# Gate logits as eight more columns of layer 2, which goes twice over the tokens

## The chip, the core and the metric

The kernel runs on one core of a Trainium2 chip. The metric is the device time of one execution in microseconds (us).

The engines are TensorE (PE in the profile; PEld is its weight load), VectorE (DVE), ScalarE (ACT), GpSimd (POOL) and SyncE (SP), which only issues transfers and reads registers here. Each works through its own instructions in order and waits for the others by semaphores.

## The reference

```python
x = attention(q, k, v)                     # sigmoid attention, 4 x 12 heads, 448 x 64 -> x: 1792 x 768
h = maximum(maximum(x @ w1, x @ w2), x @ w3)   # three projections, 768 x 768 each
y = h @ w_out                              # "layer 2", 768 x 768

logits = y @ w_gate + modality_bias[modality_id]   # 1792 x 8
e_idx = argmax(logits, axis=1)                     # one expert of eight for each token
gate = softmax(logits)[e_idx]
out[token] = gate * (relu(y[token] @ w1[e_idx]) @ w2[e_idx])   # 768 -> 1024 -> 768
```

## The kernel before

**Stages.** Attention, then the projections (`project`: six blocks of 128 output features by two halves of the tokens by three weights), then layer 2 with the routing, then the experts. There are TT = 14 token tiles of 128 tokens, and KB = 6 blocks of 128 features. h stays in SBUF as `hA`, `hB`, features on the partitions.

**Products from two parts.** Layer 2 and the experts multiply in fp32r. `split` makes a rounded copy of a tensor on ScalarE and the remainder on VectorE; a product is three matmuls: high by high, high by low, low by high.

**Gate logits.** During the projections VectorE forms `gw` = w_out @ w_gate (768 x 8) in the background. After the last projection TensorE takes `lgp` = gw^T h in plain fp32 (24 matmul calls, 32 output partitions each), VectorE copies it (`lgT`), and four transposes (`route_T`) turn it so that tokens lie on the partitions. `route_gate` adds the bias and finds expert and gate, `route_rank` counts with matmuls, `route_tiles` forms the experts' numbers of the tiles (`exid`), `route_slots` each token's slot. GpSimd then scatters the token numbers to `slots` in DRAM, in 14 indirect transfers. SyncE reads eight expert numbers from `exid` into registers; only then can it issue the loads of expert weights (`wl`).

**Layer 2.** `layer2(t)` makes 18 pairs of matmuls, 512 and 256 columns with the same weights (a tile of h, split). For the last five tiles (from T0 = 9) it first does the 512 columns of all five, and then the 256 columns of all five, so that the gather of the first 512 columns and the first splits of expert weights (`ahead`) can begin in between. The 512-column sums take the PSUM buffers a0 and a1 in turn, the 256-column sums x0 and x1.

**Stores.** A finished tile goes through one of three buffers `xo[t % 3]` to DRAM, `x2d[0]` (columns 0 to 511) and `x2d[1]` (columns 512 to 767, and the gate in column 768). All these stores, the weight loads and the reading back of `idx` are issued by SyncE, in program order. After each tile from t = 2 on, up to two loads of `wl` follow that tile's stores, until four of the fourteen are left. Two experts' weights are loaded this way: per expert w1 in three pieces and w2 in four.

Of the kernel before, what the change touches and what calls it, by code (L numbers as in the profile page):

```python
# [28 lines left out]
def attn_moe_kernel(  # L29
# [45 lines left out]
    def hold(tag, name, *shape):  # L75
        return pool.tile([128, *shape], F32, tag=tag, name=name)
# [74 lines left out]
    def ps(tag, shape, name):  # L151
        return psum.tile(shape, F32, tag=tag, name=name)
# [211 lines left out]
    with tc.manual_schedule(engines={mybir.EngineType.PE, mybir.EngineType.Activation, mybir.EngineType.DVE, SP}):  # L364
# [109 lines left out]
        def project(fb, half, wi):  # L474
# [15 lines left out]
            if half == 1:  # L490
                used[fb, wi] = step[0]

        for fb in range(KB):
            for half in range(2):
                for wi in range(3):
                    project(fb, half, wi)
                    step[0] += 1
                    background(5.8)
        step[0] += 100
        while bg or bg2:  # L500
            step[0] += 1
            background(999)


        lgp = ps("t", [128, 2, 512], "lgp")
        for kk in range(KB):
            for g in range(4):
                n = min(512, NT - 512 * g)
                nc.tensor.matmul(lgp[32 * g:32 * g + 32, 0, 0:n], gw[:, kk, :], hT[kk][:, 512 * g:512 * g + n],  # L509
                                 start=(kk == 0), stop=(kk == KB - 1))  # L510

        wo_ck = hold("P2a", "wo_ck", 2 * KB * DM)
        wo_rl = [cut(wo_ck, 0, KB, 2, 512), cut(wo_ck, KB * 2 * 512, KB, 2, DM - 512)]
        ck = [cut(wo_ck, 2 * DM * i, 2 * DM) for i in range(KB)]
        hs_ = hold("W0", "hs", 2, 2 * KB * 128)
        hs = [hs_[:, t % 2] if t < TT - 3 else hold(f"S{t - TT + 3}", f"hs{t}", 2 * KB * 128) for t in range(TT)]
        hs = [a.rearrange("p (a k c) -> p a k c", a=2, k=KB) for a in hs]
        xo_ = hold("W1", "xo", 3, XW)
        xo = [xo_[:, i] for i in range(3)]

        def split_h(t):
            for h_, k0, k1 in ((hA, 0, 4), (hB, 4, 6)):
                src = h_[:, :, 128 * t:128 * (t + 1)]
                split(hs[t][:, 0, k0:k1], hs[t][:, 1, k0:k1], src)

        def split_wo(kk):
            for w, src in zip(wo_rl, (wof[kk][:, 0:512], wof[kk][:, 512:DM])):
                split(w[:, kk, 0], w[:, kk, 1], src)

        split_wo(0)  # L530
        split_h(0)
        for kk in range(1, KB):
            split_wo(kk)
        split_h(1)
        lgT = cut(gk, 2 * DM, 512)
        nc.vector.tensor_copy(out=lgT[:, 0:256], in_=lgp[:, 0, 0:256])
        nc.vector.tensor_copy(out=lgT[0:96, 256:512], in_=lgp[0:96, 0, 256:512])


        acc_t = {}  # L540

        def layer2(t, cs=(0, 1), ks=range(KB)):
            if ks[0] == 0:
                for c in cs:
                    acc_t[t, c] = ps_a([128, 512], "acc2") if c == 0 else ps(f"x{t % 2}", [128, DM - 512], "acc2b")
            for kk in ks:
                for n, (a, b) in enumerate(((0, 0), (0, 1), (1, 0))):
                    for c in cs:
                        nc.tensor.matmul(acc_t[t, c], r(hs[t][:, a, kk, :]), r(wo_rl[c][:, kk, b]),  # L549
                                         start=(kk == 0 and n == 0), stop=(kk == KB - 1 and n == 2))  # L550

        def layer2_evac(t, cs=(0, 1)):
            o = xo[t % 3]
            if 0 in cs:
                nc.scalar.activation(out=o[:, 0:512], in_=acc_t.pop((t, 0)), func=ACTF.Copy)
            if 1 in cs:
                nc.vector.tensor_copy(out=o[:, 512:DM], in_=acc_t.pop((t, 1)))

        def layer2_store(t, cs=(0, 1)):
            o = xo[t % 3]  # L560
            if 1 in cs:
                nc.vector.tensor_copy(out=o[:, DM:DM + 1], in_=gate[:, t:t + 1])
            for c in cs:
                nc.sync.dma_start(out=x2d[c][128 * t:128 * (t + 1), :], in_=o[:, XC[c][0]:XC[c][1]])


        ro = [0]

        def tmp(*shape):
            n = 1  # L570
            for d in shape:
                n *= d
            ro[0] += n
            assert ro[0] <= 2 * DM
            return cut(gk, ro[0] - n, *shape)

        lg = tmp(TT, E)
        sh = tmp(TT, E)
        oh = tmp(TT, E)
        ohb = tmp(TT, E)  # L580
# [25 lines left out]

            return a.unsqueeze(1).to_broadcast([128, n, a.shape[1]])

        def route_T():
            for j in range(4):  # L610
                n = 128 if j < 2 else 96
                nc.tensor.transpose(lgp[:, 1, 128 * j:128 * j + n], lgT[0:n, 128 * j:128 * (j + 1)], ident[:n, :n])

        def route_gate():
            T = lgp[:, 1, :].rearrange("p (j g x) -> p g j x", j=4, g=4)
            ve.tensor_tensor(out=lg[:, 0:12].rearrange("p (g j) e -> p g j e", g=3), in0=T[:, 0:3, :, 0:E],
                             in1=bias_t[:, 0:12].rearrange("p (g j) e -> p g j e", g=3), op=ALU.add)
            ve.tensor_tensor(out=lg[:, 12:14], in0=T[:, 3, 0:2, 0:E], in1=bias_t[:, 12:14], op=ALU.add)
# [236 lines left out]
        layer2(0)  # L855
        route_T()
        split_h(2)
        layer2_evac(0)
        route_gate()
        layer2(1)  # L860
        pr, cn = route_rank()
        split_h(3)
        layer2_evac(1)
        layer2_store(0)
        layer2_store(1)
        route_tiles(cn)
        ereg = [nc.values_load(exid[0:1, i:i + 1], engines=(SP,), min_val=0, max_val=E - 1) for i in range(NSTAT)]
        wl = deque()
        for i in range(2):
            raw[i] = raw_tiles(i)  # L870
            wl.extend(load_w1(i, ereg[i]))
            wl.extend(load_w2(i, ereg[i]))

        T0 = TT - 5
        for t in range(2, TT):
            cs = (0, 1) if t < T0 else (0,)
            layer2(t, cs)
            if t + 2 < TT:
                split_h(t + 2)
            layer2_evac(t, cs)  # L880
            layer2_store(t, cs)
            if t == 2:
                route_slots(pr)
            for _ in range(2):
                if len(wl) > 4:
                    wl.popleft()()
            if t == 9:
                nc.sync.dma_start(out=idx, in_=slots.rearrange("(p c) o -> p (c o)", p=128))
        xh = hold("H1", "xh", 2 * (KB + FB) * GT)
        xt.extend(cut(xh, KB * GT * i, KB, GT) for i in range(2))  # L890
# [23 lines left out]
        for t in range(T0, TT):  # L914
            if t < TT - 1:
                layer2(t, (1,))
            else:
                layer2(t, (1,), range(0, KB - 3))
                gather_T(0, 0, "t")
                gather_T(0, 1, "x0")  # L920
                layer2(t, (1,), range(KB - 3, KB))
            layer2_evac(t, (1,))
            layer2_store(t, (1,))
            ahead(min(LA, t - T0 + 1))
# [110 lines left out]
```

## Time and profile before

| | |
|---|---|
| median of 3 runs | 766.97 us (766.82 to 767.5) |
| the profiled execution | 767.15 us, of which the trace spans 765.4 us |
| TensorE, busy share of the span | 99% |
| VectorE, ScalarE, GpSimd | 59%, 34%, 9% |
| granted clock of TensorE, mean | 0.999 |

The span runs from the first to the last instruction. Busy shares are means over stages with different limits. Matmuls are pipelined: a recorded matmul reaches past the start of the next one, so the pace of a run of matmuls is read from the chain, not from the mean duration of one. The expert stage gathers tokens by expert and works through seven full tiles and one half tile.

### The profile page before, as it was taken

To read this page: it belongs to the slowest core of one execution; us is meant where nothing else is said; L and a number is where in the kernel's file an instruction comes from. 1 tells how busy PE (TensorE), PEld (TensorE's weight loads), DVE (VectorE), ACT (ScalarE), POOL (GpSimd) and SP (SyncE) were. 2 spreads that over 40 slices of the span, in tenths; PEclk is the share of its full clock that TensorE was granted. 3 is DMA by queue.
4 is the path that set the end of the run, shared out by engine and by line. 5 is a ranking of instruction groups with operands and counts; after the bars stand their busy time and mean duration, and the time that the engine had idled before them with its cause. 6 is when DMAs were issued, how large, how long until landed. Compare 5 with 4: busy or idle time off the path is not lost.

```text
span 765.4 us, 11862 instructions
## 1 busy us (share of the span) xinstructions
PE 756.1 (99%) x4704; PEld 642.1 (84%) x4704; DVE 449.8 (59%) x754; ACT 258.1 (34%) x362; POOL 67.5 (9%) x84
## 2 busy tenths in 40 slices
PE   8999999999999999999999999999999999999996
PEld 5455544999999999999978888999999989899995
DVE  4677774757779787844137522455556555556542
ACT  4666555001010100100032222354544544454522
POOL 1000000000000000000000420313020202021010
PEclk9999999999999999999999999999999999999999
DMA  9766680132620312200001692452757211064000
GB/s 216 181 168 166 163 226 2 59 108 83 205 79 26 124 62 83 83 2 0 1 1 43 226 395 78 134 196 88 271 193 253 107 29 57 15 249 159 29 26 19
DMA packets 44993, 88.07 MB, mean 115 GB/s; under 512 B 8139, under 2 KB 27100, under 8 KB 44934
## 3 DMA queue, kind: packets, MB, share of 16 engines
q1 hardware_dynamic: 41142, 75.45, 31.2%
q0 software_dynamic: 3632, 11.59, 4.6%
q8 instruction: 39, 0.64, 0.3%
q10 hardware_dynamic: 160, 0.23, 0.1%
q14 instruction: 20, 0.16, 0.1%
HBM read 94.95 MB, written 11.57 MB: 139 GB/s over the span
## 4 chain that ended last, share of the span: by engine, by line
PE 98%; DMA 1%; issue 0%; POOL 0%; SPq 0%; POOLq 0%; DVE 0%; ACT 0%; ACTq 0%
PE acc L483 34%; PE hacc L801 16%; PE oacc L822 15%; PE acc L549 8%; PE X L336 7%; PE s L310 6%; PE acc2b L549 4%; PE X L344 1%; PE hacc L954 1%; PE xT L762 1%; PE s L326 1%; PE oh L969 1%; PE lgp L509 1%; DMA u<-in_qk_dram 1%; PE wgp L352 0%
## 5 line engine op out<-in xcount | busy, mean ns | idle before, releaser
L483 PE MATMUL acc<-xR,w_ring 128*128 128x448 f32 x864 | 210.5, 365 | 0.0
L483 PEld LDWEIGHTS acc<-xR,w_ring 128*128 128x128 f32 x864 | 162.2, 188 | 13.5 <-issue 0.7
L822 PE MATMUL oacc<-wo_ck,xh 128*128 128x512 f32 (+1 forms) x672 | 124.0, 341 | 0.0
L801 PE MATMUL hacc<-xh,wo_ck 128*128 128x256 f32 x1008 | 122.4, 283 | 0.0
L801 PEld LDWEIGHTS hacc<-xh,wo_ck 128*128 128x128 f32 x1008 | 121.9, 192 | 0.3
L822 PEld LDWEIGHTS oacc<-wo_ck,xh 128*128 128x128 f32 x672 | 102.8, 188 | 13.8
L483 PE MATMUL acc<-xLa,w_ring 128*128 128x448 f32 x360 | 102.2, 365 | 0.0
L295 ACT ACTIVATE at<-s,nlns 128x896 f32<-128x896 f32 x84 | 77.9, 1007 | 44.9 <-PE s L310 43.5
L185 DVE TENSOR_TENSOR wo_ck<-raw,wo_ck 128x512 fp32r<-128x512 f32 (+1 forms) x108 | 75.6, 743 | 6.7 <-ACT wo_ck L184 6.6
L549 PE MATMUL acc<-wo_ck,hs 128*128 128x512 f32 x252 | 77.4, 394 | 0.0
L483 PEld LDWEIGHTS acc<-xLa,w_ring 128*128 128x128 f32 x360 | 67.6, 188 | 5.3
L184 ACT ACTIVATE wo_ck<-raw 128x512 fp32r<-128x512 f32 (+1 forms) x108 | 67.1, 671 | 12.4 <-PE hacc L801 12.2
L549 PEld LDWEIGHTS acc<-wo_ck,hs 128*128 128x128 f32 x252 | 47.2, 188 | 11.3 <-ACT wo_ck L184 0.8
L549 PE MATMUL acc2b<-wo_ck,hs 128*128 128x256 f32 x252 | 56.2, 280 | 0.0
L310 PEld LDWEIGHTS s<-kq 64*128 64x128 f32 x432 | 37.6, 184 | 22.1 <-issue 15.5
L310 PE MATMUL s<-kq 64*128 64x448 f32 x432 | 51.2, 377 | 0.9 <-ACT kq L281 0.9
L465 DVE SCALAR_TENSOR_TENSOR gk<-wof,gk 128x768 f32<-128x768 f32 x48 | 45.9, 956 | 1.1
L487 ACT ACTIVATE hA<-acc 128x896 f32<-128x896 f32 x8 | 7.4, 920 | 115.1 <-PE acc L483 115.1
L808 DVE SCALAR_TENSOR_TENSOR xh<-hacc,xh 128x1024 fp32r<-128x1024 f32 x14 | 17.1, 1224 | 45.6 <-ACT xh L807 45.6
L753 POOL DMA_INDIRECT xg<-x2d,idx x30 | 30.3, 1012 | 146.8 <-PE xT L762 99.9
L549 PEld LDWEIGHTS acc2b<-wo_ck,hs 128*128 128x128 f32 x252 | 41.5, 189 | 0.1
L489 DVE TENSOR_TENSOR hB<-hB,acc 128x896 f32<-128x896 f32 x8 | 8.7, 1086 | 50.2 <-PE acc L483 50.2
(182 smaller groups left out, 700.3 us busy)
## 6 DMA issues: line engine op xcount, KB each, us to landing
raw<-in_moe_w_dram SPq DMA_DIRECT2D x24, 1024.0 KB
stage<-in_moe_w_dram SPq DMA_DIRECT2D x18, 768.0 KB
u<-in_qk_dram SPq DMA_DIRECT2D x46, 224.0 KB
raw<-in_moe_w_dram SPq DMA_DIRECT2D x12, 768.0 KB
raw_S<-in_moe_w_dram SPq DMA_DIRECT2D x12, 768.0 KB
stage<-in_moe_w_out_dram SPq DMA_DIRECT2D x6, 768.0 KB
x2d<-xo SPq DMA_DIRECT2D x14, 256.0 KB
gk<-wgT SPq DMA_DIRECT2D x8, 384.0 KB
```

The costliest lines, as they stand in the source:

```text
L184: nc.scalar.activation(out=r(dR), in_=src, func=ACTF.Copy)
L185: nc.vector.tensor_tensor(out=r(dL), in0=src, in1=dR, op=ALU.subtract)
L295: nc.scalar.activation(out=dst, in_=s[:, :, 0:S], func=ACTF.Sigmoid, scale=qscale, bias=nlns)
L310: nc.tensor.matmul(s[g][:, h, 0:S], r(kt[p, a, 0, 128 * g:128 * (g + 1)]), r(kt[p, x, 1]), start=(n == 0), stop=(n == 2))
L336: nc.tensor.matmul(X_t[u][64 * h:64 * h + 64, 0:S], vt[:, 2 * g + h], at[:, 2 * g + h], start=(g == 0), stop=False)
L465: nc.vector.scalar_tensor_tensor(out=junk, in0=wof[kb], scalar=1.0, in1=wgb[e % 2], op0=ALU.mult, op1=ALU.mult, accum_out=gw[:, kb, e:e + 1])
L483: nc.tensor.matmul(acc[:, c, 0:S], r(m[:, a, kk, :]), r(x[kk][:, c0 + S * c:c0 + S * (c + 1)]), start=(kk == 0 and n == 0), stop=(kk == KB ...
L549: nc.tensor.matmul(acc_t[t, c], r(hs[t][:, a, kk, :]), r(wo_rl[c][:, kk, b]), start=(kk == 0 and n == 0), stop=(kk == KB - 1 and n == 2))
L753: nc.gpsimd.indirect_dma_start(out=xg[i % 2][s][:, XC[c][0]:XC[c][1]], out_offset=None, in_=x2d[c], in_offset=bass.IndirectOffsetOnAxis(ap ...
L801: nc.tensor.matmul(acc[:, f], r(w[a][:, 128 * f:128 * (f + 1)]), r(x[:, kk]), start=(kk == 0 and m == 0 and f % 2 == 0), stop=(kk == KB - ...
L808: nc.vector.scalar_tensor_tensor(out=r(dL), in0=src, scalar=0.0, in1=dR, op0=ALU.max, op1=ALU.subtract)
L822: nc.tensor.matmul(dst, r(x[:, f, 128 * s:128 * (s + 1)]), r(w[a][:, c0:c1]), start=(f == 0 and m == 0 and not (shared and s == 1)), stop= ...
```

## The change

The 8 columns of `gw` are appended to the first 256 columns of w_out. Layer 2 goes twice over the tokens.

- **Pass A** (`pass_a`, tokens 0 to 13): 264 columns. ScalarE copies the 256 to `xoa` and they are stored to `x2d[0]`; VectorE adds the 8 logits to the bias in place (`lg`). The sums take x0 and x1. Split tiles of h are kept in buffers of their own; the weights for it are split in S0 to S2 during the last projections, and the other 512 columns' weights (`wo_b`) alongside.
- **Pass B** (`pass_b`, tokens 9 to 13, then 0 to 8): the other 512 columns as one matmul whose moving operand is two runs of 256. It uses the kept splits for the first five positions p and splits again for the nine others. For p = 9 to 13 it takes 256 columns of all five and then the other 256 of all five; both halves take x0 and x1. ScalarE evacuates. The routing runs beside it: `route_gate` after position 0, `route_rank` and `route_tiles` after 1, the loads of expert weights from position 3 on, two after each.
- `lgp`, `lgT` and `route_T` are gone, and the wait for the background work after the projections.

```diff
+        def split_a(i):
+            w = hold(f"S{i}", f"wo_a{i}", 2, 2, NA)              # NA = CA + E = 264
+            wo_a.extend(w[:, k] for k in range(2))
+            split(w[:, :, 0, 0:CA], w[:, :, 1, 0:CA], cut(us[i], 0, 2, DM)[:, :, 0:CA])
+            split(w[:, :, 0, CA:NA], w[:, :, 1, CA:NA], gw[:, 2 * i:2 * i + 2, 0:E])
...
                     background(5.8)
+                    if fb == KB - 1 and half == 1:
+                        split_a(wi)
+                        if wi < 2:
+                            hs1[wi] = hs_view(w_ring_[1][:, 0] if wi == 0 else hold("K1", "hs_k", 2 * DM))
+                            split_h(wi, hs1[wi])
-        lgp = ps("t", [128, 2, 512], "lgp")
-        for kk in range(KB):
-            for g in range(4):
-                n = min(512, NT - 512 * g)
-                nc.tensor.matmul(lgp[32 * g:32 * g + 32, 0, 0:n], gw[:, kk, :], hT[kk][:, 512 * g:512 * g + n],
-                                 start=(kk == 0), stop=(kk == KB - 1))
...
+        wo_b = cut(wo_ck, 0, 2, KB * 2 * CA).rearrange("p c (k a n) -> p c k a n", k=KB, a=2)
...
+        def split_b(kk):
+            split(wo_b[:, :, kk, 0], wo_b[:, :, kk, 1], wof[kk][:, CA:DM].rearrange("p (c n) -> p c n", c=2))
+        def layer2(acc, hs, w, ks=range(KB)):
+            for kk in ks:
+                for n, (a, b) in enumerate(((0, 0), (0, 1), (1, 0))):
+                    nc.tensor.matmul(acc, r(hs[:, a, kk, :]), r(w(kk, b)), start=(kk == 0 and n == 0),
+                                     stop=(kk == KB - 1 and n == 2))
+        def pass_a(t):
+            acc_t[t] = ps(f"x{t % 2}", [128, NA], "acc_a")
+            layer2(acc_t[t], hs1[t], lambda kk, b: wo_a[kk][:, b])
+        def end_a(t):
+            acc = acc_t.pop(t)
+            nc.scalar.activation(out=xoa[t % 2], in_=acc[:, 0:CA], func=ACTF.Copy)
+            nc.vector.tensor_tensor(out=lg[:, t], in0=bias_t[:, t], in1=acc[:, CA:NA], op=ALU.add)
+            nc.sync.dma_start(out=x2d[0][128 * t:128 * (t + 1), 0:CA], in_=xoa[t % 2])
...
+        for t in range(1, TT):
+            pass_a(t)
+            if t + 3 < TT:
+                split_h(t + 3, hs1[t + 3])
+            end_a(t)
+            if t % 2 == 0 and t // 2 <= KB:
+                split_b(t // 2 - 1)
...
+        toks = list(range(9, TT)) + list(range(9))
+        P0 = TT - 5
...
+        def pass_b(p, c=None, ks=range(KB)):
+            if ks[0] == 0:
+                acc_t[p] = ps_a([128, 2, CA], "acc_b") if c is None else ps(f"x{p % 2}", [128, CA], "acc_c")
+            layer2(acc_t[p], hs2[p], (lambda kk, b: wo_b[:, :, kk, b]) if c is None else lambda kk, b: wo_b[:, c, kk, b], ks)
+        def end_b(p, c=None):
+            o, rows = xo[p % 3], slice(128 * toks[p], 128 * (toks[p] + 1))
+            c0, c1 = (CA, DM) if c is None else (CA * (c + 1), CA * (c + 2))
+            nc.scalar.activation(out=o[:, c0:c1], in_=flat(acc_t.pop(p)) if c is None else acc_t.pop(p), func=ACTF.Copy)
+            if c != 1:
+                nc.sync.dma_start(out=x2d[0][rows, CA:512], in_=o[:, CA:512])
+            if c != 0:
+                nc.vector.tensor_copy(out=o[:, DM:DM + 1], in_=gate[:, toks[p]:toks[p] + 1])
+                nc.sync.dma_start(out=x2d[1][rows, :], in_=o[:, 512:XW])
+        pass_b(0)
         route_gate()
+        end_b(0)
+        pass_b(1)
         pr, cn = route_rank()
+        end_b(1)
         route_tiles(cn)
+        pass_b(2)
+        end_b(2)
         ereg = [nc.values_load(exid[0:1, i:i + 1], engines=(SP,), min_val=0, max_val=E - 1) for i in range(NSTAT)]
...
+        route_slots(pr)
+        for p in range(3, TT):
+            c = None if p < P0 else 0
+            pass_b(p, c)
+            if NK <= p + 2 < TT:                                  # NK = 5
+                split_h(toks[p + 2], hs2[p + 2])
+            end_b(p, c)
             for _ in range(2):
                 if len(wl) > 4:
                     wl.popleft()()
-            if t == 9:
+            if p == 8:
                 nc.sync.dma_start(out=idx, in_=slots.rearrange("(p c) o -> p (c o)", p=128))
```

## Rows read from the trace of the kernel before

**Rows 1.** The page, busy time of each engine and share of the span.
```profile
PE 756.1 (99%) x4704; PEld 642.1 (84%) x4704; DVE 449.8 (59%) x754; ACT 258.1 (34%) x362; POOL 67.5 (9%) x84
```
**Rows 2.** The chain that ended last, 396 to 492 us: start, length, what.
```profile
396.21 5.28 PE lgp L509 x30
...
408.05 0.39 PE lgp L612 x4
...
459.18 20.43 PE acc L549 x90
479.61 9.71 PE acc2b L549 x81
489.32 0.93 PE xT L762 x8
...
491.32 10.11 PE hacc L801 x84
```
**Rows 3.** Timeline of VectorE, 396 to 428 us: start, duration, what.
```profile
396.25 1.09 DVE L489 TENSOR_TENSOR hB<-hB,acc 128x896 f32<-128x896 f32 x1 [6.14 <-PE acc L483]
...
415.81 0.15 DVE L654 CAST gk<-rank 128x8 int32<-128x8 f32 x1
...
421.27 0.16 DVE L680 SCALAR_TENSOR_TENSOR exid<-gk 128x1 int32<-128x1 f32 x1
...
422.69 0.17 DVE L686 TENSOR_TENSOR gk<-gk 128x16 f32<-128x16 f32 x1
...
427.82 0.17 DVE L712 SCALAR_TENSOR_TENSOR spos<-gk 128x14 int32<-128x14 int32 x1
```
**Rows 4.** Groups by shape, 396 to 492 us: count, busy us, mean ns, idle before.
```profile
L185 DVE TENSOR_TENSOR hs<-hA,hs 128x512 fp32r<-128x512 f32 x14 | 9.7, 690 | 24.7 <-ACT hs L184 24.6
...
L185 DVE TENSOR_TENSOR hs<-hB,hs 128x256 fp32r<-128x256 f32 x14 | 5.9, 421 | 8.3 <-ACT hs L184 8.3
...
L184 ACT ACTIVATE hs<-hB 128x256 fp32r<-128x256 f32 x14 | 5.8, 413 | 13.1 <-PE acc2b L549 13.1
```
**Rows 5.** Timeline of SyncE's issues, 408 to 464 us.
```profile
421.46 0.26 SPq L682 DMA_DIRECT2D exd<-exid  x1
426.72 0.82 SPq L564 DMA_DIRECT2D x2d<-xo  x2
427.80 1.03 SPq L738 DMA_DIRECT2D raw<-in_moe_w_dram  x2
...
448.34 0.98 SPq L738 DMA_DIRECT2D raw<-in_moe_w_dram  x2
```
**Rows 6.** Stretches: engines' busy us, then granted clock, DMA share, GB/s.
```profile
442.00:446.00 4.00, 4.00 (x25) 3.52 (x24) 0.69 (x1) 0.63 (x1) 2.92 (x4) 1.00 1.04 411
...
458.50:459.00 0.50, 0.50 (x4) 0.41 (x4) 0.00 (x0) 0.13 (x1) 0.00 (x0) 1.00 0.51 168
```
**Rows 7.** DMA issues, 380 to 520 us: count, KB each, us to landing.
```profile
raw<-in_moe_w_dram SPq DMA_DIRECT2D x9, 1024.0 KB
raw<-in_moe_w_dram SPq DMA_DIRECT2D x6, 768.0 KB
x2d<-xo SPq DMA_DIRECT2D x14, 256.0 KB
...
x2d<-xo SPq DMA_DIRECT2D x14, 136.0 KB
...
slots<-tokid,spos POOLq DMA_INDIRECT x14, 5.8
```
**Rows 8.** Timeline of GpSimd, 395 to 500 us: first and last of 14 scatters, first gather.
```profile
428.88 1.07 POOL L715 DMA_INDIRECT slots<-tokid,spos  x1 [45.06 <-issue]
...
445.99 0.97 POOL L715 DMA_INDIRECT slots<-tokid,spos  x1 [0.30 <-issue]
...
483.36 1.00 POOL L753 DMA_INDIRECT xg<-x2d,idx  x1 [36.40 <-DVE wo_ck L185]
```
**Rows 9.** Timeline of ScalarE: the last 512-column evacuation.
```profile
479.70 0.60 ACT L555 ACTIVATE xo<-acc 128x512 f32<-128x512 f32 x1 [3.48 <-PE acc L549]
```

More of the change, by code (lines that the diff above doesn't have):

```diff
@@ L491, in project, with hs_view, split_h @@
                 used[fb, wi] = step[0]
+        CA = 256
+        NA = CA + E
+        wo_a, hs1 = [], {}
+        def hs_view(a):
+            return a.rearrange("p (a k c) -> p a k c", a=2, k=KB)
+        def split_h(t, hs):
+            for h_, k0, k1 in ((hA, 0, 4), (hB, 4, 6)):
+                src = h_[:, :, 128 * t:128 * (t + 1)]
+                split(hs[:, 0, k0:k1], hs[:, 1, k0:k1], src)
+        def split_a(i):
[3 more added lines that the diff above has]
+            split(w[:, :, 0, CA:NA], w[:, :, 1, CA:NA], gw[:, 2 * i:2 * i + 2, 0:E])
         for fb in range(KB):
@@ L498, in attn_moe_kernel @@
                     background(5.8)
[L499 to L502, printed above, removed]
-        lgp = ps("t", [128, 2, 512], "lgp")
-        for kk in range(KB):
-            for g in range(4):
-                n = min(512, NT - 512 * g)
-                nc.tensor.matmul(lgp[32 * g:32 * g + 32, 0, 0:n], gw[:, kk, :], hT[kk][:, 512 * g:512 * g + n],
-                                 start=(kk == 0), stop=(kk == KB - 1))
-        wo_ck = hold("P2a", "wo_ck", 2 * KB * DM)
@@ L513, in attn_moe_kernel @@
[L513 to L537, printed above, removed]
+                    if fb == KB - 1 and half == 1:
+                        assert not bg and not bg2
+                        split_a(wi)
+                        if wi < 2:
+                            hs1[wi] = hs_view(w_ring_[1][:, 0] if wi == 0 else hold("K1", "hs_k", 2 * DM))
+                            split_h(wi, hs1[wi])
@@ new lines, in attn_moe_kernel @@
+        wo_ck = hold("P2a", "wo_ck", 2 * KB * DM)
+        wo_b = cut(wo_ck, 0, 2, KB * 2 * CA).rearrange("p c (k a n) -> p c k a n", k=KB, a=2)
+        ck = [cut(wo_ck, 2 * DM * i, 2 * DM) for i in (0, 1, 4, 5, 2, 3)]
+        hs_w = hold("W0", "hs_w", 2, 2 * DM)
+        hs_p = hold("P1", "hs_p", 7, 2 * DM)
+        hs_r = hold("P2b", "hs_r", 2 * DM)
+        for t in range(2, TT):
+            hs1[t] = hs_view(hs_p[:, t - 2] if t < 9 else hs_w[:, t - 9] if t < 11 else ck[t - 9] if t < 13 else hs_r)
@@ L540, in attn_moe_kernel @@
+        def split_b(kk):
+            split(wo_b[:, :, kk, 0], wo_b[:, :, kk, 1], wof[kk][:, CA:DM].rearrange("p (c n) -> p c n", c=2))
         acc_t = {}
[L542 to L545, printed above, removed]
+        def layer2(acc, hs, w, ks=range(KB)):
             for kk in ks:
                 for n, (a, b) in enumerate(((0, 0), (0, 1), (1, 0))):
-                    for c in cs:
-                        nc.tensor.matmul(acc_t[t, c], r(hs[t][:, a, kk, :]), r(wo_rl[c][:, kk, b]),
-                                         start=(kk == 0 and n == 0), stop=(kk == KB - 1 and n == 2))
@@ L552, in layer2_evac @@
[L552 to L564, printed above, removed]
+                    nc.tensor.matmul(acc, r(hs[:, a, kk, :]), r(w(kk, b)), start=(kk == 0 and n == 0),
+                                     stop=(kk == KB - 1 and n == 2))
@@ new lines, in pass_a @@
+        def pass_a(t):
[6 more added lines that the diff above has]
+            nc.sync.dma_start(out=x2d[0][128 * t:128 * (t + 1), 0:CA], in_=xoa[t % 2])
+        lg = bias_t
@@ new lines, in attn_moe_kernel @@
+        split_h(2, hs1[2])
+        pass_a(0)
+        xo_ = hold("W1", "xo", 3 * XW + 2 * CA)
+        xo = [cut(xo_, XW * i, XW) for i in range(3)]
+        xoa = [cut(xo_, 3 * XW + CA * i, CA) for i in range(2)]
+        split_h(3, hs1[3])
+        end_a(0)
+        for t in range(1, TT):
[5 more added lines that the diff above has]
+                split_b(t // 2 - 1)
+        rt = hold("K1", "rt", 2 * DM)
@@ L574, in tmp @@
             assert ro[0] <= 2 * DM
-            return cut(gk, ro[0] - n, *shape)
-        lg = tmp(TT, E)
+            return cut(rt, ro[0] - n, *shape)
         sh = tmp(TT, E)
@@ L607, in bc1 @@
             return a.unsqueeze(1).to_broadcast([128, n, a.shape[1]])
[L609 to L612, printed above, removed]
         def route_gate():
[L615 to L618, printed above, removed]
             ve.tensor_reduce(out=mx, in_=lg, axis=AX.X, op=ALU.max)
@@ L854, in attn_moe_kernel @@
             nc.sync.dma_start(out=d[NT:NT + 1, :], in_=xo[0][0:1, c0:c1])
[L855 to L858, printed above, removed]
+        NK = TT - 9
+        toks = list(range(9, TT)) + list(range(9))
+        P0 = TT - 5
+        hs2 = [hs1[t] for t in toks[:NK]]
+        hs_s = [hold(f"S{i}", f"hs_s{i}", 2 * DM) for i in range(3)]
+        ring = [hs_view(a) for a in (hs_s[0], hs_s[1], hs_w[:, 0], hs_w[:, 1], hs_s[2])]
+        hs2 += [ring[i % 5] for i in range(9)]
+        def pass_b(p, c=None, ks=range(KB)):
[12 more added lines that the diff above has]
+        pass_b(0)
         route_gate()
-        layer2(1)
+        end_b(0)
+        pass_b(1)
         pr, cn = route_rank()
[L862 to L865, printed above, removed]
+        end_b(1)
         route_tiles(cn)
+        pass_b(2)
+        end_b(2)
         ereg = [nc.values_load(exid[0:1, i:i + 1], engines=(SP,), min_val=0, max_val=E - 1) for i in range(NSTAT)]
@@ L872, in attn_moe_kernel @@
             wl.extend(load_w2(i, ereg[i]))
[L874 to L883, printed above, removed]
+        route_slots(pr)
[5 more added lines that the diff above has]
+            end_b(p, c)
             for _ in range(2):
@@ L912, in ahead @@
                             ld()
-        for t in range(T0, TT):
-            if t < TT - 1:
-                layer2(t, (1,))
+        for p in range(P0, TT):
+            if p < TT - 1:
+                pass_b(p, 1)
             else:
-                layer2(t, (1,), range(0, KB - 3))
+                pass_b(p, 1, range(0, KB - 3))
                 gather_T(0, 0, "t")
                 gather_T(0, 1, "x0")
[L921 to L924, printed above, removed]
+                pass_b(p, 1, range(KB - 3, KB))
+            end_b(p, 1)
+            ahead(min(LA, p - P0 + 1))
         gather(0, ixs[0], (1,))
```

## The prediction

> **What bounds the kernel now.** I read the page first: TensorE is busy for 99% of the span [rows 1], so time can only be won by taking matmuls away and lost by letting TensorE wait. Then the chain that ended last: it is TensorE work almost from end to end, and the change touches the stretch from 396.21 (projections done, gate logits begin) to 491.32 us (first expert matmul), 95.11 us [rows 2]. In it the reader should see the gate logits (5.28 us), their transposes (0.39 us), a run of 90 matmuls of 512 columns, one of 81 matmuls of 256 columns, and the expert's 8 transposes (0.93 us). Then the DVE timeline for the routing chain [rows 3], the groups by shape for the splits [rows 4], SyncE's timeline [rows 5], DMA shares by stretch [rows 6] and issue sizes [rows 7], and GpSimd and ScalarE around the gather [rows 8, 9]. All of these hide behind TensorE today. The question is whether they still do.
>
> **TensorE's own work.** A matmul of 512 columns costs 20.43/90 = 0.2270 us and one of 256 costs 9.71/81 = 0.1199 us, weight load included [rows 2]. The slope is 0.1071/256 = 0.00042 us per column, so one of 264 is 0.1199 + 8 x 0.00042 = 0.1232 us.
> Before: 9 tiles x 18 pairs x 0.3469 = 56.2, five tiles' first 512 columns 90 x 0.2270 = 20.4, their last 256 columns 90 x 0.1199 = 10.8; 87.4 us.
> After: pass A 14 x 18 x 0.1232 = 31.05; pass B 9 x 18 x 0.2270 = 36.77; five tiles in two halves 180 x 0.1199 = 21.58; 89.4 us. That is 90 more matmuls and 8 more columns on 252: +2.0 us.
> Removed: 5.28 + 0.39 = 5.67 us. The rank matmuls, the expert's transposes and small pacing losses stay. Net -3.7 us.
> Not in this trace: pass B's moving operand is two runs of 256 columns that lie apart. Its bounds are one matmul of 512 (0.2270) and two of 256 (0.2398): 0 to +2.1 us. I take 0, as it is one instruction with one weight load.
>
> **Small waits on TensorE.** (a) The third pair of 264-column weights is split on DVE behind the last projection maximum, which ends near 397.3 [rows 3]. Its subtraction (512 wide 0.69, then 16 wide about 0.15 [rows 3, 4]) is done near 398.1; pass A's fourteenth matmul wants it at 396.21 + 13 x 0.1232 = 397.8. About +0.35 us. (b) In the five split tiles both halves now use the buffers x0 and x1. The last first half (p=13) and the first second half (p=9) both take x1, so TensorE waits for one evacuation: a 256-wide ScalarE copy (0.41 [rows 4]) and the hand-over each way, together about +0.6 us. Before, the 512-column half had other buffers. Sum so far: -3.7 + 0.95 = -2.7 us.
>
> **The splits.** Nine tiles are split a second time, and all of pass A's splits sit beside 2.22 us passes. One tile costs DVE 0.69 + 0.42 = 1.1 us [rows 4], with the logit add (about 0.15) and every other step a weight split (0.7): at most 2.0 of 2.22 us. Hidden. If that cover went, the excess would be paid 14 times.
>
> **Routing.** It now starts after pass A, at about 396.2 + 31.05 + 0.35 = 427.6, and pass B sets its cover. The gate chain takes some 4 us (it leads up to the rank matmuls, which come after two passes of 18 x 0.2270 = 4.09: 8.2 us), so the rank matmuls don't wait. From their end, 436.4, the tiles chain takes 421.27 - 415.81 + 0.16 = 5.6 us and the slots chain 427.82 - 422.69 + 0.17 = 5.3 us [rows 3]: 442.2 and 447.5. Queued behind it on DVE is the split for p=5, done at 448.6; its low part is first wanted near 449.0. Just hidden: a slip of 0.5 us costs that slip.
>
> **The loads and stores on SyncE's queue.** This is the step that decides. Before, SyncE sends the expert numbers at 421.46, reads eight registers until the next store at 426.72, and issues the first weight load at 427.80; the tenth goes out by 449.3 [rows 5]. They are six of 1024 KB and four of 768 KB, 9.44 MB [rows 7]. A tile's pair of loads (about 1.9 MB) and its stores (256 + 136 KB) come every 6.24 us, which the DMA engines keep up with: they run full and fall idle near 458.8 [rows 6]. That is 11.4 MB (ten loads, five tiles' stores) in 31 us, 0.367 MB per us from the first load on, scatters included.
> After: exid is ready at 442.2, the stores of p=2 and the register reads (5 us) last to 448.4, the second store of p=3 waits for DVE until 448.9, and the first load goes out at 449.6. A pair now comes with every pass of 4.09 us, but 2.1 to 2.4 MB need 5.2 to 6.4 us. So a backlog grows, and the stores of x2d stand in it: SyncE issues them on the same queue, each behind the loads of the tiles before it.
> Store p=8 (its first part) has 9.44 MB of loads, four tiles' stores (1.08) and its own 0.13 ahead: 10.65 MB / 0.367 = 29.0 us, so its data end at 478.6 and it lands at about 479.6. Store p=7 has 8.29 MB: 22.6 us, landed about 473.2.
> What waits: xo has three buffers. ScalarE's evacuation of p=10's first half writes where store p=7 reads, p=11's where store p=8 reads. Unhindered, the first halves (18 x 0.1199 = 2.16 us) would end at 467.2, 469.3, 471.5, 473.7 and 475.8. p=12 needs p=10's PSUM buffer: free at 473.2 + 0.45 instead of 469.9, so it starts 2.1 us late. p=13 needs p=11's: free at 479.6 + 0.4 = 480.0 instead of a start at 473.7. TensorE is then 6.3 us late in all. Before, the same three buffers wait for nothing, since the last load has landed by 459 and the five halves follow.
> Bounds: DMA at the fullest stretch's 0.411 MB per us [rows 6] gives 25.9 us instead of 29.0 and a wait of 3.2 us; a rate a tenth lower gives 9. I take the measured mean. If a store doesn't stand behind the loads on its queue, the wait is nothing.
> The Trainium skill, "DMA: Bandwidth & Descriptors", section "Queues, rings and completion order", says that each DMA engine consumes the descriptors of a ring in ring order and that SyncE's row has one ring on each engine. By that rule the stores wait as worked out above and the sum is +3.6 us; if they could overtake, it would be -2.7. No row here shows the order of a store and a load; the rows show only that one backlog exists.
>
> **The gather.** The scatters begin at 447.5 + 0.9 = 448.4, last 18.1 us and land 5.8 later [rows 7, 8], about 472; the slot list is then read behind the backlog, near 480. The gather starts 483.36 - 479.61 = 3.75 us after the last first half and the transposes 5.96 us after that [rows 2, 8], of which some is slack. With p=13 ending at 482.2 the gather starts near 486 and the transposes are due at 482.8 + 9.7 = 492.5. Hidden with half a microsecond to spare by that full distance. ScalarE's evacuations are 0.60 us before and shorter after [rows 9].
>
> **Sum.** -3.7 + 0.95 + 6.3 = +3.6 us: 767.15 + 3.6 = 770.7 for an execution like the profiled one, which is 0.2 above the median of the runs: 770.5.
>
> **Rivals.**
> 1. Stores overtake loads, or land in time. Then only TensorE's work counts: 767.0 - 2.7 = 764.3, from 763.2 (no waits at all) to 766.4 (two-run operand at its upper bound). For it: ScalarE never waits for a store in this trace. Against: the backlog is 5 MB here and was under 2 MB there. It decides as soon as store p=8 lands before 473.3 instead of 479.6, that is, with 6.3 us less of backlog.
> 2. The wait is half as large, because the DMA runs at its best rate or the loads go out some microseconds sooner: 767.0 - 2.7 + 3.2 = 767.5. No measurable change.
> 3. The wait costs TensorE its clock as well. It would stand idle for 2.1 and some 4.2 us with 2.2 us of work between. The granted clock is 1.00 in every row here [rows 6] and TensorE has no such gap in this stretch. If the clock fell to its lower level for 2 to 5 us of the work that follows, that work doubles: 772.5 to 775.5. The Trainium skill, "TensorE: Matmul & The Clock Gate", Part 1, has idleness throttle the array to 1.2 GHz; no run here shows it.
> 4. Each added matmul pays an exposed weight load: 90 x about 0.1 = +9 us more. Against it: the 256-column run above already holds one weight load per matmul at 0.1199 us. I leave it 1 in 100.
>
> **Chances.** Forecast (full wait) 0.58; rival 1 0.22; rival 2 0.12; rival 3 0.07; rival 4 0.01. The full wait's own range is 768.3 to 772.0. Taken together 8 in 10 lie between 763.6 and 772.5. A measurement of this kernel tells 0.2% (1.5 us) from no change: faster means under 765.4, slower above 768.5. Rival 1 gives 0.22 less the upper end of its operand cost, rival 2 a little on both sides: faster 0.24, same 0.16, slower 0.60.
>
> **What would show it.** In the profile after: no gate-logit matmuls; 252 matmuls of 264 columns at about 0.123 us each; first load near 449.6; DMA full until about 478; ScalarE standing before the evacuations of p=10 and p=11 for several microseconds with no engine to wait for, and TensorE idle twice between 471 and 480. If TensorE runs through that stretch, the order of the queue is not what I took, and the time is near 764. If the wait sits earlier, at p=5, DVE's routing chain was too long; if at the transposes, the gather was.

## The result and the profile after

| | median us (range, runs) | ratio to before [95% interval] |
|---|---|---|
| before | 767.06 (766.82 to 767.50, 5) | |
| changed | 773.31 (772.13 to 776.44, 5) | 1.0088 [1.0068, 1.0108] |

The change makes the kernel 0.9% slower, 6.25 us by the medians and 2.8 us more than predicted. The profiled execution took 772.55 us. Its span is 770.3 us against 765.4, and its mean granted clock 0.994 where it had been 0.999.

The chain that ended last, of the kernel after (start, length, what):

```profile
397.77 29.21 PE acc_a L546 x239
426.98 8.18 PE acc_b L546 x36
...
435.73 17.65 PE acc_b L546 x78
...
457.49 11.32 DMA x2d<-xo
...
468.88 10.75 DMA x2d<-xo
...
479.73 0.39 ACT xo L872
...
480.17 3.66 PE acc_c L546 x18
...
484.34 9.98 PE acc_c L546 x81
494.32 0.87 PE xT L762 x8
...
496.26 3.77 PE hacc L801 x31
```

The first expert matmul starts at 496.26 and not at 491.32 [rows 2]: 4.94 us, which is the whole difference of the spans. Two stores of x2d (of p = 6 and p = 8), 22 us together, now stand in a chain that was TensorE work almost from end to end. Who waits for them is in ScalarE's timeline (in brackets the idle time before, and what ended it). These are the first halves' evacuations p = 9, 10 and 11:

```profile
468.92 0.38 ACT L872 ACTIVATE xo<-acc_c 128x256 f32<-128x256 f32 x1 [3.00 <-DMA x2d<-xo]
...
473.85 0.38 ACT L872 ACTIVATE xo<-acc_c 128x256 f32<-128x256 f32 x1 [3.72 <-DMA x2d<-xo]
...
479.73 0.38 ACT L872 ACTIVATE xo<-acc_c 128x256 f32<-128x256 f32 x1 [4.68 <-DMA x2d<-xo]
```

TensorE's timeline has the first halves p = 11, 12 and 13 and then the second halves, each behind one of these evacuations, or (the last) behind the turn of x1:

```profile
469.35 2.42 PE L546 MATMUL acc_c<-wo_ck,hs_s 128*128 128x256 f32 x18 [0.63 <-ACT xo L872]
474.28 3.81 PE L546 MATMUL acc_c<-wo_ck,hs_w 128*128 128x256 f32 x18 [2.51 <-ACT xo L872]
480.17 3.65 PE L546 MATMUL acc_c<-wo_ck,hs_w 128*128 128x256 f32 x18 [2.07 <-ACT xo L872]
484.34 6.74 PE L546 MATMUL acc_c<-wo_ck,hs_s 128*128 128x256 f32 x54 [0.52 <-ACT xo L872]
```

The same 18 matmuls take 2.42 us at 469 and 3.8 us at 474 and at 480. The stretches say why (TensorE's busy time and matmuls; then granted clock, DMA share, GB/s):

```profile
472.00:474.00 2.00, 0.00 (x0) 1.00 1.04 424
474.00:476.00 2.00, 1.72 (x8) 0.51 1.03 412
476.00:478.00 2.00, 2.00 (x12) 0.64 1.04 377
478.00:480.00 2.00, 0.10 (x1) 1.00 0.31 109
480.00:482.00 2.00, 1.83 (x11) 0.72 0.26 90
482.00:484.00 2.00, 1.81 (x9) 0.50 0.14 47
```

After each of the two long pauses the granted clock falls to 0.5, that is from 2.4 to 1.2 GHz; after the pause of 0.63 us the 18 matmuls still take 2.42 us. And the DMA engines, which had been idle from 459 on [rows 6], are full until 478.

SyncE's timeline: the first loads, the slowest pair, the last pair, and the store of p = 8:

```profile
448.73 1.03 SPq L738 DMA_DIRECT2D raw<-in_moe_w_dram  x2
...
453.95 3.44 SPq L745 DMA_DIRECT2D raw<-in_moe_w_dram  x2
...
466.79 1.77 SPq L738 DMA_DIRECT2D raw<-in_moe_w_dram  x2
468.88 0.34 SPq L874 DMA_DIRECT2D x2d<-xo  x1
```

The first load goes out 20.9 us later than before [rows 5], and the store of p = 8 right behind the last two.

### The profile page after: what moved, and what is told of

It is laid out like the page before. It is cut to its first block, busy times and chain, and to the rows that moved or that the text cites. A ratio compares the mean times of both kernels' runs of the same rounds, so it can differ in the third digit from the quotient of the medians.

```text
span 770.3 us, 12019 instructions
## 1 busy us (share of the span) xinstructions
PE 755.4 (98%) x4742; PEld 649.6 (84%) x4742; DVE 455.9 (59%) x768; ACT 270.5 (35%) x399; POOL 66.8 (9%) x84
## 4 chain that ended last, share of the span: by engine, by line
PE 94%; DMA 3%; issue 0%; ACT 0%; DVE 0%; POOL 0%; SPq 0%; POOLq 0%; ACTq 0%
PE acc L483 34%; PE hacc L801 16%; PE oacc L822 15%; PE X L336 7%; PE s L310 6%; PE acc_a L546 4%; PE acc_b L546 3%; DMA x2d<-xo 3%; PE acc_c L546 2%; PE X L344 1%; PE hacc L970 1%; PE s L326 1%; PE xT L762 1%; PE oh L985 1%; DMA u<-in_qk_dram 1%
## 5 line engine op out<-in xcount | busy, mean ns | idle before, releaser
L336 PE MATMUL X<-at,u 128*64 128x448 f32 x192 | 37.8, 544 | 0.0
L766 DVE TENSOR_TENSOR xh<-xT,xh 128x512 fp32r<-128x512 f32 x21 | 14.4, 691 | 37.1 <-ACT xh L765 37.1
L489 DVE TENSOR_TENSOR hA<-hA,acc 128x896 f32<-128x896 f32 x16 | 17.4, 1086 | 31.1 <-PE acc L483 30.7
L852 POOL MEMSET xo<- 128x784 f32 x3 | 2.1, 757 | 387.2 <-DVE hs_p L185 387.2
L361 DVE CAST xR<-X 128x448 fp32r<-128x448 f32 x24 | 14.9, 620 | 34.7 <-PE X L344 34.7
```

Of the source, the lines that this page charges most:

```text
L336: nc.tensor.matmul(X_t[u][64 * h:64 * h + 64, 0:S], vt[:, 2 * g + h], at[:, 2 * g + h], start=(g == 0), stop=False)
L489: nc.vector.tensor_tensor(out=dst, in0=dst, in1=acc[:, :, 0:S], op=ALU.max)
```

## The experiments

**Which runs can be compared.** The first four kernels ran on a chip on which the kernel before itself took 772.16 us (769.90 to 775.73, 23 runs). Everywhere else it took 767.0 to 767.4, so the ratios of those four aren't used. All four were run again on other chips (labels with b, below "second"), and the conclusions rest on these. Theory: the stores stand behind the weight loads on SyncE's queue, the three `xo` buffers come free late, TensorE waits, and the clock falls in the waits. Rivals: the bytes have to move in any case, so another order only shifts the wait; or the clock costs nothing, since it falls while TensorE would wait anyway.

**Two marks.** The kernel before, and the changed kernel, each run as a kernel beside others, on two different chips.

> The kernel before, unchanged, run beside the changed one on this chip. No theory is at stake: it should take about 767.0 us, 5 us less than the changed kernel, at a granted clock of 0.999, and it gives the mark that the two kernels below have to pass.

> The changed kernel as it is, on the same chip as the three below, to settle what they are measured against: on one chip so far its profile had no wait of ScalarE for TensorE's signal at 457 to 468, on another four kernels with the same first half of pass B had one of 7 to 8 us. Theory, the difference is the chip's or the execution's: 772 to 774 here, with the waits for the stores of p = 6, 7 and 8 as in the profile after. If the kernel before is near 772 on a chip where the hold-back kernel is at 768, the whole stretch is slower there for both kernels.

Before: 767.41 us (766.73 to 768.90, 11), ratio 1.0005 [0.9996, 1.0014]. Changed: 774.41 us (771.74 to 777.89, 6), ratio 1.0084 [1.0070, 1.0099]. The change costs the same here, and its executions lie 6 us apart where those of before lie 2 apart (3.4 on the chip of the changed kernel, 766.38 to 769.74, 17).

### 1. The stores of the second quarter issued by ScalarE

```diff
-                nc.sync.dma_start(out=x2d[0][rows, CA:512], in_=o[:, CA:512])
+                nc.scalar.dma_start(out=x2d[0][rows, CA:512], in_=o[:, CA:512])
```

> The stores of columns 256 to 511 in pass B are issued by ScalarE instead of SyncE; all else is as in the changed kernel. Theory (a store waits in its queue behind the weight loads issued before it): on a queue without loads they land 2 to 4 us after they are issued, TensorE stands still no more between p=11 and p=13, the clock stays at 1.00 and the time is 764.3, between 763.8 and 765.5. Rival 1 (the 16 DMA engines are full until 478, so any store is late on any queue): much of the wait stays, 767 to 772. Rival 2 (the pair of PSUM buffers x0 and x1, or the late routing, makes the wait): 773 as before the edit.

> The stores of the second quarter issued by ScalarE, so that they don't stand behind weight loads, beside a kernel before at 767. Theory: the first halves no longer wait, as in the run before; but idx and the stores of the last third stay behind the loads on SyncE, the gather comes late, and of the 6.3 us at most 2 to 3 come back: 769 to 771. If the order behind the loads were not the cause, 772 to 774 as the changed kernel.

First chip 771.16 us (769.33 to 773.26, 12). Second 768.27 us (767.30 to 770.64, 12), ratio 1.0015 [1.0005, 1.0025]: 5 us under the changed kernel by the ratios, 6 by the medians, though nothing but the issuing engine differs. TensorE goes from the first halves to the second ones with one wait of 0.47 us; it waits later, for the gathered tokens (TensorE's timeline of the second run, whose profiled execution, 770.55 us, was one of the slower ones):

```profile
489.13 0.33 PE L762 MATMUL xT<-ident,xg 128*128 128x128 f32 x1 [2.19 <-DMA xg<-x2d,idx]
491.26 1.53 PE L762 MATMUL xT<-ident,xg 128*128 128x128 f32 x7 [1.81 <-DMA xg<-x2d,idx]
```

The place behind the loads on SyncE is the cause of the first waits. The edit takes the stores out of two places at once, from behind the loads in the queue and from behind SyncE's own waiting issues (see the last section), and doesn't tell one from the other. In this execution 4 us come back as a wait for the gather; what the gather waits for last is `idx`, which SyncE issued at 476.18 and which landed at 484.47. The time missed both expectations: it is above the 764.3 of the first and under the 769 to 771 of the second. It lies in the range of rival 1 (767 to 772), which is right in part: the store of p = 8, issued by ScalarE at 467.17, landed at 473.5, after 6.3 us and not 2 to 4, where on SyncE it landed at 479.6.

### 2. Buffers of their own for the five first halves

```diff
-        rt = hold("K1", "rt", 2 * DM)
+        rt = hold("K1", "rt", 3 * DM)
...
+            d = o[:, c0:c1] if c != 0 else h0[p - P0]
-            nc.scalar.activation(out=o[:, c0:c1], ...
+            nc.scalar.activation(out=d, ...
-                nc.sync.dma_start(out=x2d[0][rows, CA:512], in_=o[:, CA:512])
+                nc.sync.dma_start(out=x2d[0][rows, CA:512], in_=d[:, 0:CA])
...
+        h0 = [cut(rt, 2 * DM + CA * i, CA) for i in range(3)] + xoa
```

> The five first halves are evacuated into five buffers of their own (256 columns each) instead of into xo; every store stays on SyncE's queue, as late as it is. Theory (the late stores cost time only because ScalarE may not write xo before they have read it): no wait in the first halves; what is left is the gather, which has to wait for the last of these stores near 480 and then has 6 us until the transposes fall due near 486: 764.3 to 765.5. Rival 1 foretells the same here. Rival 2: 773 as before the edit.

> The five buffers of their own for the first halves and nothing else: ten loads, stores behind them as in the changed kernel. Theory, late stores hurt through the buffers alone: no first half waits though its predecessors' stores land as late as before, TensorE runs through to the second halves, 764 to 765.5. Rival, the late stores hold up the gather as well: in the changed kernel the last second halves came late themselves; here they come 6 us sooner, and if the stores of the second halves then stand behind what is left of the loads, xT waits for xg and 767 or more is left. The waits of ScalarE for xo of p = 4 and 5 (evacuations p = 7 and 8) stay in either case.

First chip 767.37 us (766.62 to 769.55, 6). Second 766.18 us (765.90 to 770.07, 11), ratio 0.9997 [0.9986, 1.0008]. The stores are as late as ever, and no first half waits. What is left in TensorE's timeline is the turn of x1 and, again, the gather:

```profile
475.80 6.74 PE L546 MATMUL acc_c<-wo_ck,hs_s 128*128 128x256 f32 x54 [0.47 <-ACT xo L873]
...
486.25 0.33 PE L762 MATMUL xT<-ident,xg 128*128 128x128 f32 x1 [0.48 <-DMA xg<-x2d,idx]
488.04 0.98 PE L762 MATMUL xT<-ident,xg 128*128 128x128 f32 x7 [1.46 <-DMA xg<-x2d,idx]
```

So a late store costs through the buffer that it holds, and with that gone through the gather: both sides of the expectation were partly right.

### 3. Idle matmuls in the two long pauses

```diff
             c = None if p < P0 else 0
+            if p >= TT - 2:
+                if p == TT - 2:
+                    idle = ps("t", [128, 2, 512], "idle")
+                for i in range(20 if p == TT - 2 else 28):
+                    nc.tensor.matmul(idle[:, 0, 0:CA], r(hs2[9][:, 0, 0, :]), r(wo_b[:, 0, 0, 0]), start=True, stop=True)
             pass_b(p, c)
```

> TensorE gets 20 matmuls of 256 columns that nobody reads before the first half of p=12 and 28 before that of p=13, about as long as it stands there (2.8 and 3.6 us); stores and buffers as in the changed kernel. If what goes beyond the wait of 6.3 us is the clock that falls while TensorE stands: the clock stays near 1.00, the time falls to 770.5 (769.8 to 771.2) and the runs lie within 0.7 us of each other. If the excess and the scatter of the runs come from the stores themselves: 772 to 776 as before the edit, at a clock near 1.00. If the filler only lengthens TensorE's work: above 776.

> The idle matmuls in the two pauses again, beside the changed kernel. If the fallen clock is part of the time of the changed kernel: granted clock 0.998 to 0.999, and 1 to 1.8 us under the changed kernel. If the pauses alone set the time: the same as the changed kernel within 0.5 us. If the idle matmuls outlast the waits in most executions: up to 2 us over it in its fastest ones.

Nothing is removed; TensorE only has work in the pauses. First chip 772.71 us (772.23 to 774.00, 12). Second 771.94 us (770.88 to 773.68, 6), ratio 1.0062 [1.0047, 1.0077], beside the changed kernel's 774.41 and 1.0084: with 48 more matmuls 2.5 us less by the medians and 1.7 by the ratios, whose intervals overlap a little. The same stretches as above, of the second run, and pieces of its chain:

```profile
474.00:476.00 2.00, 2.00 (x17) 1.00 1.03 420
...
480.00:482.00 2.00, 2.00 (x17) 1.00 0.13 46
482.00:484.00 2.00, 2.00 (x18) 1.00 0.36 123
```

```profile
399.62 29.21 PE acc_a L546 x239
...
481.87 2.42 PE acc_c L546 x18
...
484.80 9.98 PE acc_c L546 x81
...
496.72 3.29 PE hacc L801 x27
```

The clock stays at 1.00. This execution is 1.85 us late before the stretch begins (pass A's long piece starts at 399.62, in the profile after at 397.77). Counted from there, ScalarE's evacuation of p = 11 comes after 81.81 us here (at 481.43) and after 81.96 there (479.73), so the waits stayed; but the first expert matmul comes after 97.10 us instead of 98.49. That saving, 1.4 us between these two executions, is the clock's. The rival "the clock costs nothing" falls.

### 4. Seven loads beside pass B, not ten

```diff
-                if len(wl) > 4:
+                if len(wl) > 7:
```

> The three loads of the second expert's w1 (3.1 MB) are not issued during pass B but with the remaining loads in the expert stage, so 7 loads instead of 10 stand in the queue. Theory: 3.1 MB less are ahead of store p=8, it lands some 8 us sooner, near 471, just as ScalarE wants its buffer; no wait: 764.3 to 765.0. Rival 1 foretells the same. Rival 2: 773 as before the edit. If the second expert's weights then come too late, the loss shows as a wait near 527 us.

> Seven loads in pass B and not ten, as before. Order of the queue: after the first expert's seven loads the queue is free, the stores of p = 7 and later land within some 3 us, and nothing in the first halves waits: TensorE's sum with the turn of x1, 764.5 to 765.5 where TensorE's signal comes on time, some 2.5 us more where it comes late as in the run before. Amount of bytes: 767 to 768 in either case, because the held-back loads then delay the second expert.

The other three loads go out during the first expert. First chip 767.89 us (766.91 to 770.02, 6). Second 765.74 us (764.86 to 767.98, 12), ratio 0.9980 [0.9970, 0.9990]: 8.7 us under the changed kernel on the same chip, 1.4 under before, and just above the 764.5 to 765.5 expected. The last store in the way lands early enough for two short waits only (ScalarE's timeline of the second run, p = 9 and 10):

```profile
471.39 0.38 ACT L872 ACTIVATE xo<-acc_c 128x256 f32<-128x256 f32 x1 [2.67 <-DMA x2d<-xo]
...
473.97 0.38 ACT L872 ACTIVATE xo<-acc_c 128x256 f32<-128x256 f32 x1 [1.37 <-DMA x2d<-xo]
```

TensorE waits 0.59 and 0.17 us behind them. The three loads that were held back delay nobody: that profile has no wait of TensorE after 490 us.

### 5. One load after each pass

```diff
-            for _ in range(2):
+            for _ in range(1):
```

> One weight load after each of the passes p = 3 to 12 in place of two after each of p = 3 to 7: the same ten loads of up to 1 MiB, spread over twice the time, so that a store never stands behind more than one of them (1 MiB at the 411 GB/s of the windows is 2.6 us). Theory, order of the queue: every store lands within some 5 us of its issue, its buffer is needed 12 us later, so no evacuation of the first halves waits, TensorE's 6.3 us of pauses go, and the clock has no pause in which to fall: about 5 to 6 us under the changed kernel, 766 to 767, with the granted clock at 0.999. Rival, amount of bytes: the ten loads have to move anyway and the last of them, issued at about 476 instead of 468, pushes idx, the gather and the second expert's splits later: the time stays at 771 to 773, with TensorE waiting for xT or for the splits instead. Open from the runs before: TensorE's pause of 2 to 3 us at about 466 to 469, in which ScalarE waited for TensorE's signal of pass p = 7; if it comes from the full DMA engines it goes here, and 764 to 765 is left.

> One load after each pass as in the kernel with one load, the first halves evacuated into five buffers of their own, and their accumulators in the two large PSUM buffers instead of x0 and x1, so that no first half waits for the evacuation of the one two before. Theory: all of the waits in the stretch that the change brought are gone; what is left is the sum of TensorE's work, 3.7 us under the kernel before, plus 0.35 for the first split: 763.5 to 765. Rival, amount of bytes or a late gather: 767 or more, with TensorE waiting for xT. If it stays at 767 with a pause at 466 to 469, that pause has nothing to do with the stores or the buffers.

773.93 us (771.80 to 774.23, 5), ratio 1.0085 [1.0071, 1.0099]; with the buffers of 2 and other PSUM buffers (the edit is in 6) 772.69 us (772.31 to 773.45, 5), ratio 1.0074 [1.0060, 1.0088]. My theory failed on both. In the second one TensorE runs without a pause to the last second half, and then stands (its timeline):

```profile
491.52 0.47 PE L762 MATMUL xT<-ident,xg 128*128 128x128 f32 x1 [6.42 <-DMA xg<-x2d,idx]
493.00 1.75 PE L762 MATMUL xT<-ident,xg 128*128 128x128 f32 x7 [1.00 <-DMA xg<-x2d,idx]
```

SyncE's timeline shows that the last four loads were not spread:

```profile
470.41 0.34 SPq L907 DMA_DIRECT2D idx<-slots  x1
...
471.48 0.39 SPq L745 DMA_DIRECT2D raw0b<-in_moe_w_dram  x1
...
472.57 0.39 SPq L738 DMA_DIRECT2D raw<-in_moe_w_dram  x1
...
473.73 0.39 SPq L738 DMA_DIRECT2D raw<-in_moe_w_dram  x1
...
474.89 0.54 SPq L738 DMA_DIRECT2D raw<-in_moe_w_dram  x1
```

The read of `idx` waits there for the scatters until 470.41, everything behind it on SyncE waits too, and then four loads go out in 3.4 us with the stores of the first halves between and behind them. The DMA engines are full from 476 to 484 (410 and 387 GB/s in stretches of 4 us). The last of these stores, issued at 475.86, moves from 484.0 to 486.9 by its packets, and the first gather, which needs it, starts at 488.11 instead of 483.36 [rows 8]. The rival, that the bytes only move the wait, is right for this order. How much of it is the bunching, and how much that the last loads go out this late in any case (about 476 was expected), no run separates: the read of `idx` was not moved.

### 6. Both remedies, and other PSUM buffers

```diff
-... if c is None else ps(f"x{p % 2}", [128, CA], "acc_c")
+... if c is None else ps_a([128, CA], "acc_c") if c == 0 else ps(f"x{p % 2}", [128, CA], "acc_c")
```

> Seven loads and the first halves' accumulators in the two large PSUM buffers, without buffers of their own: it splits the 2.3 us between the hold-back kernel (765.74) and the one with both (763.45). If they are the turn of x1 alone, predicted at 0.6: 765.1 with the waits of about 0.6 for the stores of p = 6 and 7 still there, 763.5 if the turn was all.

> Seven loads, the five buffers of their own for the first halves, and their accumulators in the two large PSUM buffers. Theory: 0.6 us under the hold-back kernel (the turn of x1 gone), 764.0 to 765.0, under the kernel before by 2 to 3 us; the gather in time, since the last store is not behind a load. Rival, a late gather as in the kernel with one load per pass: 767 or more, with xT waiting for xg.

Seven loads with the PSUM edit: 764.93 us (763.96 to 767.07, 11), ratio 0.9972 [0.9963, 0.9981]; against 0.9980 for seven loads alone that is 0.6 us for the turn of x1, as expected, though the two intervals overlap. With the buffers of 2 as well: **763.45 us (763.10 to 766.49, 6), ratio 0.9958 [0.9942, 0.9974]**, under both kernels. Its chain has TensorE alone from the routing to the first expert:

```profile
436.71 28.68 PE acc_b L546 x126
465.40 20.51 PE acc_c L546 x171
485.91 0.87 PE xT L762 x8
486.78 1.07 PE acc_c L546 x9
487.85 10.13 PE hacc L801 x84
```

## Why the prediction was wrong in its number and right in its mechanism

- **TensorE's own work, -3.7 us: right.** The kernel without waits is 767.12 - 763.45 = 3.7 us under before; -3.7 + 0.35 was predicted for it. From the end of the projections to pass B are 426.98 - 395.92 = 31.06 us, where 31.05 + 0.35 was predicted; TensorE's pause for the third pair of weights is 0.30. Pass B's matmul with two runs of columns takes 8.18/36 = 0.2272 us as one run does [rows 2]: the value taken, 0, holds, and the bound of 2.1 us is out. Rival 4 is out with it: a matmul of pass A takes 29.21/239 = 0.1222 us.
- **Small waits: right.** The turn of x1 is 0.52 us in the profile; experiment 6 agrees (0.6, within its noise).
- **Splits and routing hidden: right.** The rank matmuls end at 435.7 (436.4 predicted), the first load goes out at 448.73 (449.6).
- **The stores behind the loads: right, in place and size.** The evacuations that waited are p = 10 and 11, at 473.85 and 479.73; worked out were 473.2 and 479.6 for the landings. Only the short wait at p = 9, behind the store of p = 6 (0.63 us on TensorE), was not forecast. That the second landing came out to the tenth is partly luck: the first load went out 0.9 us sooner than worked out, and from it to the landing (479.62) were 30.9 us and not 30.0. The packets of the second-quarter stores move between those of the loads, in the order of issue (us, from the trace's packets):

```
store of p   4            5            6            7            8
moves        456.2-456.9  461.4-463.4  465.9-468.1  471.0-473.2  476.8-479.0
```

  The Trainium skill, "DMA: Bandwidth & Descriptors", section "Queues, rings and completion order", says that descriptors are consumed in ring order; the trace agrees. Experiment 1 moves these stores to another queue, and the waits go. Not in the prediction is that a part of the wait lies ahead of the queue: the result of p = 8 was ready at 465.1, but SyncE issued its store at 468.88, which is 3.8 of the 14.5 us until it landed.
- **What failed is the sum, which left the clock out.** Two pauses of 2.1 and some 4 us with 2.2 us of work between were in the forecast, and the clock's fall in them was rival 3 with a chance of 0.07, as if it were another case. In this run each of the two pauses was followed by a fall. In the profiled execution the 18 matmuls of p = 13 took 3.66 us in the chain, where experiment 3's chain has 2.42 at full clock (+1.2); the 81 second halves take 9.98 us in both and lost nothing. 769.0 of span from the sum, plus 1.2, is 770.2; 770.3 was measured. The fall after the first pause costs nothing, since p = 13 waits for the store of p = 8 anyway. Of the 2.8 us by the medians that is the part which this trace explains; of the rest, the device time is 2.25 us longer than the span here and 1.75 before, and the median lies 0.8 above the profiled execution.

  In other executions the clock costs more. The chain of the changed kernel's slowest one (777.89 us, mean clock 0.987):

```profile
400.58 29.21 PE acc_a L546 x239
...
483.11 4.22 PE acc_c L546 x18
...
487.84 11.94 PE acc_c L546 x81
```

  Against experiment 3's chain the two later pieces are 3.8 us longer, and the clock is still 0.50 at 490 us. That is rival 3's place and price: forecast and rival 3 were one case, at 772.5 to 775.5. The Trainium skill, "TensorE: Matmul & The Clock Gate", Part 1, says that idleness throttles the array to 1.2 GHz; that is what these rows show. Not all of the scatter is this: the same execution starts pass A's long piece 2.8 us later than the profile after (400.58, 397.77), far ahead of the pauses; its clock was 0.88 and 0.95 in the first two stretches of 10 us.
- **The gather with half a microsecond to spare: right for this order, and the next wait once it is undone.** In the changed kernel the transposes don't wait. As soon as TensorE is no longer late (experiments 1, 2 and 5), they do: 4.0, 1.9 and 7.4 us. Rival 1's price, 764.3 with the stores out of the way, left this wait out; experiment 1 measured 768.27.

What stays open: why executions of the same kernel lose so unequally to the clock, in the pauses and at the start, and what is slower on the first chip.

## What to carry to other kernels

When routing or any other source of a load burst moves later, list everything that the same queue issues behind the burst, and follow each store to the buffer that it holds: here the loads in front of two stores, with the fall of the clock and the turn of x1, cost 10 us (773.31 against 763.45) where the change itself saves 3.7. In these runs the long pauses on TensorE carried a fall of the clock with them: price the two as one case. Keeping back the loads that nobody needs yet was the cheapest remedy (one number in the code); spreading them failed here, where a waiting issue in the same program order bunched the last four again.

## What the hardware showed that I had not expected

- **Issuing waits too.** In this program each transfer of SyncE waits for the one that last signalled the same semaphore, eight transfers before: the store of p = 6 landed at 468.81, and the store of p = 8, eight transfers later, went out at 468.88. With full DMA engines two loads took 3.44 us to issue (1.03 at the start), and that held up the stores behind them before they reached the queue.
- **One of sixteen parts lands late.** A transfer's landing is signalled in sixteen parts. In the profile after, fifteen parts of a load came between 459.92 and 460.30, the sixteenth at 461.60; of the next between 461.80 and 462.09, the last at 463.56. The waiting engine starts with the last. The two stores that TensorE waited for land so too: fifteen parts by 472.29 and 478.09, the sixteenth at 473.74 and 479.62, and ScalarE's evacuations start at 473.85 and 479.73. So 1.5 us of each wait was for one part.
- **A late signal on one chip.** In all four profiles of the first chip ScalarE's evacuation of p = 7 stood 4 to 9 us, until 463.9 to 469.2, and TensorE after it, with gaps inside one tile's matmuls. Here the kernel of experiment 4 there, ScalarE and then TensorE:

```profile
469.20 0.60 ACT L872 ACTIVATE xo<-acc_b 128x512 f32<-128x512 f32 x1 [7.17 <-issue]
```

```profile
467.63 0.28 PE L546 MATMUL acc_c<-wo_ck,hs_s 128*128 128x256 f32 x1 [0.21 <-issue]
469.03 5.21 PE L546 MATMUL acc_c<-wo_ck,hs_s 128*128 128x256 f32 x40 [1.12 <-issue]
```

  In three of the four the signal that it waited for last, by the semaphore that the trace names, was TensorE's, whose recorded matmuls of that pass end near 462; in the fourth the view names a store. Those traces lack records in this stretch (some landings have 5 or 6 of their sixteen parts), so a part of the picture may be the record's. None of the profiles on other chips has such a wait. Its cause was not found.
